# Decoding all of w_out inside the first stage's blocks 1 to 7 and parting it in block 8

## The chip, the cores and the metric

The kernel runs on one core of one Trainium2 chip. The metric is the time of one execution on the device in microseconds. PE is TensorE, DVE is VectorE, ACT is ScalarE, POOL is GpSimd; SP only issues DMAs here.

## What is computed

```python
def _attn_ref(q, k, v):                  # 8 batches, 8 heads, 576 tokens, 64 dims
    k_p, v_p = (mean over 8 neighbouring tokens of k, v)
    attn = softmax(q @ k_p.T / sqrt(D))
    return attn @ v_p                    # laid out as x: 4608 x 512
def _moe_ref(x, w_in, w_out):            # d_ff 2048
    h = x @ w_in
    return (h * cos(h)) @ w_out
def _moe2_ref(x, w_in, w_out, g_ln):     # d_ff 1024
    h = x @ w_in
    e = exp(h - max(h)); sm = e / (sum(e) + 1e-9)
    solu = h * sm
    ln = (solu - mean(solu)) / sqrt(var(solu) + 1e-6) * g_ln
    return ln @ w_out
```

The weights come as float64 bit patterns and are decoded on the chip.

## The kernel before

**Stages.** Stage 1 walks over 9 blocks of 512 tokens (`NB`). In each block it multiplies the block's attention output x with w_in in 8 units (`NQ`); one unit (`h_mm`, L619) is 24 matmuls of 512 columns, dealt out over 8 slots (`SL`) of 3 matmuls. A block has therefore 64 slots, and the attention of the next block is laid between them. Stage 2 (`y_mm`, L702) walks over the same 72 units: 42 matmuls of 256 columns each, seven products of a Strassen-like scheme, from h cos h (called g) and combinations of w_out (`w_op`). Stage 3 is the second feed-forward layer. Every f32 matmul is done as three matmuls of a rounded high part and a low part, so every operand is first parted: ACT rounds (`hi`), POOL or DVE subtracts (`lo`).

**The order is written by hand.** `work[slot]` is a table of what is issued behind each slot; `put_at(j)` puts something at a slot counted from the start of block j-1 (its first argument may run past a block's end). Each engine then runs its own instructions in that order and waits, in order, for what each needs; an engine may run ahead of the others as far as its data allow.

**The chain of a unit** (`chain`, L624). After unit n's matmuls: step 0, ACT, L630, scale to int; step 1, DVE, L633; step 2, ACT, L636, sine; step 3, DVE, L638, the product with h, which also frees the unit's PSUM. Three units' h are held in PSUM, so unit n+3 can't start until step 3 of unit n is done. `g_store` then writes the result to DRAM (gd). Within unit n: step 2 and step 3 of unit n-2 at slots 0 and 4, step 0 and step 1 of unit n-1 at slots 0 and 3, the store at slot 6.

**The attention between the slots** (`Attn.plan`). Eight score matmuls at slots 0, 3, ... 21, whose row maximum and difference (`less`, DVE, L399 and L400) stand two slots behind; two rounds of exponentials on ACT at 12 and 24, each of which makes ACT load a table before it and another before the next sine; row sums and reciprocals on DVE (`norm`: L476, L479, L480) at 15 and 27; `prep_v` (POOL, ACT, then DVE's L344 to L349) at 19, 22, 25 in the blocks in which a batch begins; transposes and the product with v from 27 on, with their low parts on DVE (L527, L510, L552). Scores, transposes and the product share two PSUM tiles.

**Decoding.** A `Chunk` is 128 x 512 float64 words: a load, two ACT operations (`s1`), three DVE operations (`bits`: L119, L123, L127), one POOL addition (`join`, L139). Eight chunks of the second layer's w_in and the first half of w_out (8 chunks) are decoded from block 1 on, one every 24 slots; their four sums per pair of chunks (L839, DVE), the rounding (L163, ACT) and the subtraction (L164, POOL) follow at once, and the parted operands go to DRAM. The second half of w_out is decoded, summed and parted in block 8, while the first half is fetched back; the last chunk runs over into stage 2. Stage 2 takes g back from DRAM (`g_load`, L653), makes four sums of it on DVE (`g_sums`, L664), and parts it (`g_split`, L675 ACT, L677 DVE). Of that, the first unit's is put at slots 57 and 60 of block 8, the second's behind the last unit.

## Time and profile before

| | |
|---|---|
| time, median of 3 runs (lowest, highest) | 1376.14 us (1375.66, 1377.78) |
| the profiled execution: its time, and its span on the core | 1375.22 us, 1373.4 us |
| PE busy | 1307.3 us, 95% of the span |
| DVE, ACT, POOL busy | 77%, 51%, 37% |

The span begins with the first instruction and ends with the last; 1.8 us of the execution lie around it. Busy matmuls are modelled at their ends, so PE's share is not a share of its peak. Stage 1 with its attention of block 0 takes the first 579 us, stage 2 runs from 584 to 960 us, stage 3 from there to the end.

### The profile page before, as it was taken

What the parts mean: (1) busy time and instruction counts of PE and PEld (TensorE: products, weight loads), DVE (VectorE), ACT (ScalarE), POOL (GpSimd) and SP (SyncE); (2) the same over time, 40 slices, a digit from 0 to 9 for tenths busy, and PEclk for the clock granted to TensorE, in tenths of its full rate; (3) what the DMA queues carried; (4) which work ended last, traced back from release to release, by engine and by line L of the source; (5) the groups of instructions that cost most, each with busy time, mean ns of one, the idle gap of its engine ahead of it and who ended that gap; (6) DMA issues with size and microseconds to landing.
All of it is one profiled execution on the core that took longest, in us unless ns stands there. A gap on an engine that the chain in (4) does not pass through costs nothing. (4 is left out here: it accounts for less than half of the span.)

```text
span 1373.4 us, 20471 instructions
## 1 busy us (share of the span) xinstructions
PE 1307.3 (95%) x7510; PEld 1136.8 (83%) x7510; DVE 1054.4 (77%) x1686; ACT 700.4 (51%) x1000; POOL 503.4 (37%) x676
## 2 busy tenths in 40 slices
PE   5879899999999989879999999999999999999998
PEld 4558788787877878779999999999878888888887
DVE  7897677867778675898889888887677777776753
ACT  4576656655566564744444444443444444444432
POOL 3757555756466240621110000111234333333310
PEclk8989999999999999979999999999999999999999
DMA  8424456555465526944455555558521011111101
GB/s 291 153 81 170 157 189 216 200 216 187 155 209 193 185 103 224 348 154 136 144 152 170 162 166 153 158 150 291 233 63 62 31 62 34 60 39 54 40 23 39
DMA packets 80116, 200.83 MB, mean 146 GB/s; under 512 B 7696, under 2 KB 26128, under 8 KB 80016
## 3 DMA queue, kind: packets, MB, share of 16 engines
q1 hardware_dynamic: 79872, 199.52, 43.1%
q8 instruction: 59, 0.97, 0.3%
q14 instruction: 41, 0.34, 0.1%
q10 hardware_dynamic: 144, 0.00, 0.0%
HBM read 122.95 MB, written 76.55 MB: 145 GB/s over the span
## 5 line engine op out<-in xcount | busy, mean ns | idle before, releaser
L619 PE MATMUL h<-x,w 128*128 128x512 f32 x1728 | 440.9, 403 | 21.9 <-DVE t L638 17.7
L619 PEld LDWEIGHTS h<-x,w 128*128 128x128 f32 x1728 | 318.7, 191 | 90.6 <-DVE t L638 19.7
L702 PE MATMUL y<-g,wy 128*128 128x256 f32 x3024 | 367.9, 285 | 13.2 <-DVE g L677 6.1
L702 PEld LDWEIGHTS y<-g,wy 128*128 128x128 f32 x3024 | 366.7, 194 | 14.5 <-DVE g L677 6.8
L675 ACT CAST g<-gs 128x1024 fp32r<-128x1024 f32 x72 | 75.7, 1051 | 175.2 <-PE y L702 106.9
L677 DVE TENSOR_TENSOR g<-gs,g 128x1024 fp32r<-128x1024 f32 x72 | 89.5, 1243 | 41.1 <-ACT g L675 41.1
L139 POOL TENSOR_TENSOR dec<-dec,raw 128x512 int32<-128x512 int32 x24 | 34.6, 1440 | 233.0 <-DVE dec L127 218.9
L633 DVE SCALAR_TENSOR_TENSOR t<-t,h 128x1024 f32<-128x1024 int32 x72 | 87.4, 1214 | 22.2 <-ACT t L630 22.1
L636 ACT ACTIVATE t<-t,cst 128x1024 f32<-128x1024 f32 x72 | 82.9, 1152 | 37.8 <-DVE t L633 37.7
L910 POOL TENSOR_TENSOR yl<-yr,yh 128x1024 fp32r<-128x1024 f32 x18 | 43.6, 2420 | 148.7 <-ACT yh L905 148.7
L630 ACT ACTIVATE t<-h 128x1024 int32<-128x1024 f32 x72 | 73.2, 1017 | 47.6 <-PE h L619 47.3
L231 POOL TENSOR_TENSOR kvraw<-kvraw 128x256 f32<-128x256 f32 (+3 forms) x128 | 81.6, 637 | 29.3 <-DMA kvraw<-in_vM 11.1
L638 DVE TENSOR_TENSOR t<-t,h 128x1024 f32<-128x1024 f32 x72 | 86.8, 1206 | 0.0
L664 DVE TENSOR_TENSOR gs<-gr,gs 128x256 f32<-128x256 f32 x144 | 72.5, 503 | 5.0
L677 DVE TENSOR_TENSOR g<-gr,g 128x768 fp32r<-128x768 f32 x72 | 72.3, 1005 | 0.0
L1041 POOL TENSOR_TENSOR sc<-sc,cst 128x1 f32<-128x1 f32 x36 | 20.3, 565 | 140.8 <-DVE sc L1030 113.5
L139 POOL TENSOR_TENSOR wf<-dec,raw 128x512 int32<-128x512 int32 x24 | 32.3, 1345 | 105.5 <-DVE dec L127 82.7
L1076 ACT COPY o<-o 128x512 f32<-128x512 f32 x36 | 21.1, 586 | 96.7 <-PE o L1094 96.7
L1092 PE MATMUL o<-w,lh 128*128 128x512 f32 x176 | 69.0, 392 | 0.0
L1094 PE MATMUL o<-w,ll 128*128 128x512 f32 x176 | 68.5, 389 | 0.0
L1093 PE MATMUL o<-w,lh 128*128 128x512 f32 x176 | 68.5, 389 | 0.0
L675 ACT CAST g<-gr 128x768 fp32r<-128x768 f32 x72 | 59.8, 830 | 0.0
(181 smaller groups left out, 2545.4 us busy)
## 6 DMA issues: line engine op xcount, KB each, us to landing
gd<-t SPq DMA_DIRECT2D x72, 512.0 KB, 2.9
gr<-gd SPq DMA_DIRECT2D x72, 512.0 KB, 4.0
raw<-in_w_in SPq DMA_DIRECT2D x24, 512.0 KB, 5.3
raw<-in_w_out SPq DMA_DIRECT2D x24, 512.0 KB, 5.1
kvraw<-in_kT SPq DMA_DIRECT2D x32, 288.0 KB, 4.4
qT<-in_qT SPq DMA_DIRECT2D x36, 256.0 KB, 4.6
yd<-yo SPq DMA_DIRECT2D x36, 256.0 KB, 4.8
yr<-yd SPq DMA_DIRECT2D x18, 512.0 KB, 4.1
```

The costliest lines, as they stand in the source:

```text
L231: nc.gpsimd.tensor_tensor(out=x[:, 0:m], in0=x[:, 0:m], in1=x[:, m:2 * m], op=ALU.add)
L619: nc.tensor.matmul(h_ps[n][:, i], lhsT=w[:, a, kk, :], rhs=x[:, b], start=(kk == 0 and m == 0), stop=(kk == KD - 1 and m == 2),)
L630: nc.scalar.activation(out=t.bitcast(I32), in_=h, func=AF.Copy, scale=1.0 / TWO_PI, bias=0.25)
L633: nc.vector.scalar_tensor_tensor(out=t, in0=t.bitcast(I32), scalar=-TWO_PI, in1=h, op0=ALU.mult, op1=ALU.add)
L636: nc.scalar.activation(out=t, in_=t, func=AF.Sin, bias=halfpi)
L638: nc.vector.tensor_tensor(out=t, in0=t, in1=h, op=ALU.mult)
L664: nc.vector.tensor_tensor(out=o, in0=x, in1=y, op=ALU.subtract)
L675: nc.scalar.copy(out=flat(g[-1])[:, 0:n * NH], in_=flat(f)[:, 0:n * NH])
L677: nc.vector.tensor_tensor(out=flat(g[-1])[:, 0:n * NH], in0=flat(f)[:, 0:n * NH], in1=flat(g[-2])[:, 0:n * NH].bitcast(F32), op=ALU.subtract)
L702: nc.tensor.matmul(y_ps[j][i][:, NH * c:NH * (c + 1)], lhsT=w[:, a, P * c:P * (c + 1)], rhs=g[y][b], start=(q == 0 and c == 0 and k == 0), ...
L1092: nc.tensor.matmul(ps, lhsT=hi, rhs=w[:, 0], start=(c == 0), stop=False)
L1093: nc.tensor.matmul(ps, lhsT=hi, rhs=w[:, 1], start=False, stop=False)
```

## The change

All 16 chunks of w_out are now decoded before block 8, each 16 slots after the one before it (24 chunks in all, from block 1's start). Their values in f32 (`wf`) and the four sums of each pair (`w_sums`, L835 of the new file) go to DRAM unparted. In block 8 `w_load` fetches six of the eight groups back and `w_split` rounds them on ACT and subtracts on POOL, group after group at slots 4, 11, 18, 25, 32 and 42; the last two groups are loaded and parted in stage 2. The sums and the parting of stage 2's first g unit stand at slots 52 and 58, the sums of the second at 56, its parting behind the last unit. The steps of the unit chain and the attention's operations are moved by a slot or a few, and the decoding of the second layer's w_out in stage 2 begins 5 units later with 7 units between chunks in place of 8.

```diff
         def plan(self, put, o, raw, ahead=10):
             put(o - ahead, self.load, raw)
             put(o, self.s1)
-            put(o + 2, self.bits)
-            put(o + 4, self.join)
+            put(o + 4, self.bits)
+            put(o + 7, self.join)
...
-                    staged((o, o + 2), self.scores, p, u)
-                put((12, 12, 24, 24)[p], self.exp, p)
+                    staged((o, o + 3), self.scores, p, u)
+                put((13, 13, 25, 25)[p], self.exp, p)
             for b in new:
-                staged((19, 22, 25), prep_v, b)
+                staged((14, 17, 21), prep_v, b)
             for hf in range(2):
-                o = (15, 27)[hf]
-                staged((o, o + 2), self.norm, 2 * hf, 2 * hf + 1)
+                o = (16, 28)[hf]
+                staged((o, o + 3), self.norm, 2 * hf, 2 * hf + 1)
...
-    def w_done(q, kept):
+    def w_sums(q):
+        a11, a12, a21, a22 = (w_f[2 * q + 1 - i % 2][:, NH * h:NH * (h + 1)] for i, h in (
+            (0, 0), (1, 0), (0, 1), (1, 1)))
+        s = w_s[q] = wo.tile([P, 4, NH], F32, "ws")
...
+            put(o + 9, lambda: nc.sync.dma_start(out=wf[2 * q][:, 1 - f % 2], in_=w_f[f]))
+            if f % 2:
+                put(o + 10, w_sums, q)
+                put(o + 13, lambda: nc.sync.dma_start(
+                    out=wf[2 * q + 1].rearrange("p a (b n) -> p (a b) n", n=NH), in_=w_s[q]))
...
+    def w_load(q):
+        if q < 6:
+            w_s[q] = [xp.tile([P, 2, BLK], F32, tag="x0", name="ws") for _ in range(2)]
...
+        for t, d in zip(w_s[q], (wf[2 * q + 1], wf[2 * q])):
+            nc.sync.dma_start(out=t, in_=d)
+
+    def w_split(q, put, o):
...
+        for i in range(4):
+            two(put, o + i, lambda i=i: part(i, 0), lambda i=i: part(i, 1), lambda i=i: src(i))
...
-        for q in range(4):
-            chunks += w_chunks(q, False)
+        chunks += [w_chunk(f) for f in range(NF)]
         put = put_at(2)
         for i, c in enumerate(chunks):
-            c.plan(put, 3 * SL * (i + 2 * (i // NQ)), raws[i % 2])
+            c.plan(put, 2 * SL * (i + 2 * (i // NQ > 0)), raws[i % 2])
         for k in range(KH):
-            o = 3 * SL * KD * (k + 1) + 13
+            o = 2 * SL * KD * (k + 1) + 3
             put(o, weight_sums, k)
...
-        for i, c in enumerate(sum((w_chunks(q, True) for q in range(4, NQ)), [])):
-            c.plan(put, (2, 15, 22, 31, 38, 46, 52, 58)[i], raws[i % 2], 8 if i < 7 else 7)
-        for i in range(16):
-            put(4 + 7 * i // 2, w_fetch, *divmod(i, 4))
-        put(57, g_sums, 0)
-        put(60, g_split, 0)
+        for q, o in enumerate((4, 11, 18, 25, 32, 42)):
+            put(o - 9, w_load, q)
+            w_split(q, put, o)
+        for m in range(2):
+            put(44 + 2 * m, g_load, m)
+            put(52 + 4 * m, g_sums, m)
+        put(58, g_split, 0)
...
-                if n > 1 and s in (0, 4):
-                    chain(n - 2, 2 + s // 4)
-                if n > 0 and s in (0, 3):
-                    chain(n - 1, s // 3)
-                if n > 1 and s == 6:
+                if n > 1 and s == 3:
+                    chain(n - 2, 3)
+                if n > 0 and s in (0, 4, 7):
+                    chain(n - 1, (0, 4, 7).index(s))
+                if n > 1 and s == 5:
                     g_store(n - 2)
...
-        for n, step in ((last - 1, 2), (last, 0), (last - 1, 3), (last, 1), (last, 2)):
+        for n, step in ((last - 1, 3), (last, 0), (last, 1), (last, 2)):
             chain(n, step)
         g_load(2)
-        g_sums(1)
         g_store(last - 1)
+        g_split(1)
         chain(last, 3)
         g_store(last)
...
-                lambda o, fn, *a, i=i: late[NQ * i + 3 + o // 3].append(lambda: fn(*a)), 6,
+                lambda o, fn, *a, i=i: late[8 + 7 * i + o // 3].append(lambda: fn(*a)), 6,
```

Three places in the engines' order.

DVE in the middle of block 2. Before, from the preparation of v (vw, vL) to the low part of the first transpose (eT); L633 and L638 are steps 1 and 3 of the chain, of two units that follow each other (L638's is the older):

```order
L344 TENSOR_TENSOR vw<-v,vw 128x128
L345 TENSOR_SCALAR vw<-vw,cst 128x128
L347 SCALAR_TENSOR_TENSOR vw<-vw,cst 128x128
L349 TENSOR_TENSOR vL_101<-vw,cst 128x512
L633 SCALAR_TENSOR_TENSOR t<-t,h 128x1024
L476 TENSOR_REDUCE sm<-e 128x8 x2
L479 TENSOR_SCALAR sm<-sm 128x16
L480 RECIPROCAL sm<-sm 128x16
L638 TENSOR_TENSOR t<-t,h 128x1024
L527 TENSOR_TENSOR eT<-eTp,eT 128x512
```

Now, the same stretch (the last `less`, L399 and L400, is now behind the preparation of v):

```order
L344 TENSOR_TENSOR vw<-v,vw 128x128
L345 TENSOR_SCALAR vw<-vw,cst 128x128
L347 SCALAR_TENSOR_TENSOR vw<-vw,cst 128x128
L349 TENSOR_TENSOR vL_101<-vw,cst 128x512
L399 TENSOR_REDUCE mx<-sc 128x4
L400 TENSOR_TENSOR e<-sc,mx 128x288
L638 TENSOR_TENSOR t<-t,h 128x1024
L633 SCALAR_TENSOR_TENSOR t<-t,h 128x1024
L476 TENSOR_REDUCE sm<-e 128x8 x2
L479 TENSOR_SCALAR sm<-sm 128x16
L480 RECIPROCAL sm<-sm 128x16
L527 TENSOR_TENSOR eT<-eTp,eT 128x512
```

L638 has moved from behind the younger unit's L633 and the row sums to ahead of both. In blocks 4 to 7 the four additions of `w_sums` stand just ahead of this L638.

ACT in block 7 from its second exponentials on; before:

```order
L457 ACT_TABLE_LOAD
L457 ACTIVATE e<-e 128x576 x2
L114 ACTIVATE dec<-raw 128x512
L115 ACTIVATE raw<-raw 128x512
L526 CAST eT<-eTp 128x512
L509 CAST eL<-eLp 128x512
L636 ACT_TABLE_LOAD
L636 ACTIVATE t<-t,cst 128x1024
```

Now, from the row ahead of the exponentials' L630 on:

```order
L114 ACTIVATE dec<-raw 128x512
L115 ACTIVATE raw<-raw 128x512
L636 ACTIVATE t<-t,cst 128x1024
L630 ACTIVATE t<-h 128x1024
L457 ACT_TABLE_LOAD
L457 ACTIVATE e<-e 128x576 x2
L526 CAST eT<-eTp 128x512
L636 ACT_TABLE_LOAD
L636 ACTIVATE t<-t,cst 128x1024
```

The sine (L636) of the unit that PE needs next, and the chunk's `s1` (L114, L115), now stand ahead of the exponentials.

DVE at the end of block 8 (t_5173, t_5229, t_5288 before and t_5190, t_5225, t_5265 now are the chain tiles of the last three units, 69, 70 and 71; gs, gr and g belong to stage 2's first two units). Before:

```order
L664 TENSOR_TENSOR gs_5240<-gr_5106 128x512
L664 TENSOR_TENSOR gs_5240<-gr_5106,gs_5240 128x256 x2
L633 SCALAR_TENSOR_TENSOR t_5229<-t_5229,h_5168 128x1024
L638 TENSOR_TENSOR t_5173<-t_5173,h_5108 128x1024
L119 TENSOR_SCALAR dec_5249<-dec_5249 128x512
L123 TENSOR_SCALAR dec_5249<-dec_5249 128x512
L127 SCALAR_TENSOR_TENSOR dec_5249<-raw_558,dec_5249 128x512
L677 TENSOR_TENSOR g_5268<-gs_5240,g_5266 128x1024
L677 TENSOR_TENSOR g_5272<-gr_5106,g_5270 128x768
L638 TENSOR_TENSOR t_5229<-t_5229,h_5168 128x1024
L633 SCALAR_TENSOR_TENSOR t_5288<-t_5288,h_5224 128x1024
```

Now:

```order
L664 TENSOR_TENSOR gs_5227<-gr_5179,gs_5227 128x256 x2
L677 TENSOR_TENSOR g_5239<-gs_5206,g_5237 128x1024
L677 TENSOR_TENSOR g_5243<-gr_5167,g_5241 128x768
L638 TENSOR_TENSOR t_5190<-t_5190,h_5140 128x1024
L633 SCALAR_TENSOR_TENSOR t_5225<-t_5225,h_5186 128x1024
L638 TENSOR_TENSOR t_5225<-t_5225,h_5186 128x1024
L633 SCALAR_TENSOR_TENSOR t_5265<-t_5265,h_5221 128x1024
L677 TENSOR_TENSOR g_5274<-gs_5227,g_5272 128x1024
L677 TENSOR_TENSOR g_5278<-gr_5179,g_5276 128x768
L638 TENSOR_TENSOR t_5265<-t_5265,h_5221 128x1024
```

The parting of the first g unit now stands ahead of unit 69's last step, the parting of the second ahead of unit 71's last step, and no decoding stands between them. On PE the order of all matmuls is unchanged; the third product of stage 2's first unit waits, now as before, for unit 71's L638, because its PSUM bank held that unit's h.

## Rows read from the trace of the kernel before

**Rows 1.** The page: busy time of PE and the others.

```profile
PE 1307.3 (95%) x7510; PEld 1136.8 (83%) x7510; DVE 1054.4 (77%) x1686; ACT 700.4 (51%) x1000; POOL 503.4 (37%) x676
```

**Rows 2.** PE's h matmuls, blocks 1 to 7: busy, mean | idle before, releaser.

```profile
L619 PE MATMUL h<-x,w 128*128 128x512 f32 x1328 | 340.9, 402 | 15.4 <-DVE t L638 15.2
```

**Rows 3.** PE in order of time, blocks 2 and 7: start, us, ... [idle before].

```profile
212.22 1.65 PE L619 MATMUL h<-x,w 128*128 128x512 f32 x6 [1.09 <-DVE t L638]
213.71 0.49 PE L522 MATMUL eTp<-ident,em 128*128 128x128 f32 x3
...
506.48 1.80 PE L619 MATMUL h<-x,w 128*128 128x512 f32 x5 [3.53 <-DVE t L638]
```

**Rows 4.** DVE in order of time, middle of block 2.

```profile
204.54 1.24 DVE L344 TENSOR_TENSOR vw<-v,vw 128x128 fp32r<-128x128 f32 x1
...
208.06 1.21 DVE L633 SCALAR_TENSOR_TENSOR t<-t,h 128x1024 f32<-128x1024 int32 x1
...
211.00 1.16 DVE L638 TENSOR_TENSOR t<-t,h 128x1024 f32<-128x1024 f32 x1
212.08 0.68 DVE L527 TENSOR_TENSOR eT<-eTp,eT 128x512 fp32r<-128x512 f32 x1
```

**Rows 5.** The sums of w_out (L839) in blocks 1 to 7, four groups of four.

```profile
122.00:530.00 408.00, 9.28 (x16) 0.99 0.52 183
```

**Rows 6.** Stretches: length, busy PE, PEld, DVE, ACT, POOL; clock, DMA, GB/s.

```profile
50.00:100.00 50.00, 35.50 (x152) 26.65 (x151) 45.95 (x69) 33.64 (x49) 34.84 (x34) 0.90 0.30 104
330.00:335.00 5.00, 5.00 (x22) 4.31 (x21) 2.95 (x3) 1.29 (x3) 4.83 (x8) 0.67 0.86 311
500.00:510.00 10.00, 6.47 (x27) 4.98 (x27) 9.04 (x15) 6.74 (x10) 5.80 (x8) 0.87 0.13 52
585.00:590.00 5.00, 0.89 (x4) 0.89 (x5) 4.96 (x5) 0.95 (x2) 2.19 (x1) 0.50 0.61 210
595.00:600.00 5.00, 5.00 (x28) 5.00 (x27) 4.93 (x6) 4.74 (x9) 4.50 (x4) 0.55 0.88 272
```

**Rows 7.** PE in order of time from block 8 into stage 2.

```profile
529.40 50.03 PE L619 MATMUL h<-x,w 128*128 128x512 f32 x219
584.04 0.80 PE L702 MATMUL y<-g,wy 128*128 128x256 f32 x2 [4.61 <-ACT g L675]
589.11 2.51 PE L702 MATMUL y<-g,wy 128*128 128x256 f32 x10 [4.27 <-DVE g L677]
594.07 6.45 PE L702 MATMUL y<-g,wy 128*128 128x256 f32 x32 [2.45 <-issue]
602.00 1.22 PE L702 MATMUL y<-g,wy 128*128 128x256 f32 x8 [1.49 <-DVE g L677]
```

**Rows 8.** DVE, then ACT, in order of time around the same place.

```profile
578.13 1.77 DVE L664 TENSOR_TENSOR gs<-gr 128x512 f32<-128x512 f32 x1 [1.58 <-POOL wf L139]
...
592.75 1.21 DVE L638 TENSOR_TENSOR t<-t,h 128x1024 f32<-128x1024 f32 x1
...
603.92 1.22 DVE L677 TENSOR_TENSOR g<-gs,g 128x1024 fp32r<-128x1024 f32 x1
605.06 0.95 DVE L677 TENSOR_TENSOR g<-gr,g 128x768 fp32r<-128x768 f32 x1
605.93 0.68 DVE L664 TENSOR_TENSOR gs<-gr 128x512 f32<-128x512 f32 x1
...
582.21 1.05 ACT L675 CAST g<-gs 128x1024 fp32r<-128x1024 f32 x1 [0.35 <-DVE gs L664]
583.16 0.83 ACT L675 CAST g<-gr 128x768 fp32r<-128x768 f32 x1
583.90 1.15 ACT L636 ACTIVATE t<-t,cst 128x1024 f32<-128x1024 f32 x1
584.95 1.00 ACT L630 ACTIVATE t<-h 128x1024 int32<-128x1024 f32 x1
```

**Rows 9.** ACT's group of the chunks' first step, 529 to 585 us.

```profile
L114 ACT ACTIVATE dec<-raw 128x512 f32<-128x512 f32 x8 | 5.3, 666 | 13.5 <-DMA raw<-in_w_out 13.5
```

More of the change, by code (lines that the diff above doesn't have):

```diff
@@ L150, in plan @@
             put(o, self.s1)
-            put(o + 2, self.bits)
-            put(o + 4, self.join)
+            put(o + 4, self.bits)
+            put(o + 7, self.join)
             if self.g is not None:
-                put(o + 7, lambda: nc.vector.tensor_scalar(
+                put(o + 10, lambda: nc.vector.tensor_scalar(
                     out=self.f, in0=self.f, scalar1=self.g, scalar2=None, op0=ALU.mult))
@@ L667, in tile @@
         def tile():
[L668 to L669 removed]
+            if m < 2:
+                return (wo, wi)[m].tile([P, 4, NH], F32R, "g", (12, 9)[m] + len(g))
             return xp.tile([P, 4, NH], F32R, tag=("x0", "x1")[m % 2], name="g")
@@ L747, in fused_kernel @@
     whole, tw, w2_in_t, w2_out_t = {}, {}, [], []
-    wd = [dram.tile([P, 2, BLK], F32R, tag="wd", name=f"wd{i}", bufs=40) for i in range(36)]
-    wd_in, wd_out, wd_tw, wd_y = wd[0:8], wd[8:16], wd[16:24], wd[24:36]
-    wd_y4 = [dram.tile([P, 2, NH], F32R, tag="wd4", name=f"wd4{i}", bufs=4) for i in range(4)]
+    wd = [dram.tile([P, 2, BLK], F32R, tag="wd", name=f"wd{i}", bufs=24) for i in range(24)]
+    wd_in, wd_out, wd_tw = wd[0:8], wd[8:16], wd[16:24]
+    wf = [dram.tile([P, 2, BLK], F32, tag="wf", name=f"wf{i}", bufs=16) for i in range(16)]
     def whole_tile(c):
@@ L785, in tile @@
                 return t[0]
-            two(put, o + 9, lambda: tile()[:, 0], lambda: tile()[:, 1], lambda: c.f)
-            put(o + 15, put_away, d, tile)
+            two(put, o + 12, lambda: tile()[:, 0], lambda: tile()[:, 1], lambda: c.f)
+            put(o + 18, put_away, d, tile)
         return done
@@ L866, in w_fetch @@
-    def w_fetch(q, i):
-        if i == 0:
-            w_get[q] = w_slots(q)
-        t = w_get[q][i]
-        if i < 3:
-            nc.sync.dma_start(
-                out=t.rearrange("p o w n -> p o (w n)").bitcast(F32), in_=wd_y[3 * q + i].bitcast(F32))
-        else:
-            nc.sync.dma_start(out=t.bitcast(F32), in_=wd_y4[q].bitcast(F32))
-    w_get = {}
-    def w_chunks(q, kept):
-        return [
-            Chunk(w_out_w[2 * q], lambda *a: None, whole=lambda: w_whole(2 * q)),
-            Chunk(w_out_w[2 * q + 1], w_done(q, kept), whole=lambda: w_whole(2 * q + 1))]
+    def w_sums(q):
+        a11, a12, a21, a22 = (w_f[2 * q + 1 - i % 2][:, NH * h:NH * (h + 1)] for i, h in (
+            (0, 0), (1, 0), (0, 1), (1, 1)))
+        s = w_s[q] = wo.tile([P, 4, NH], F32, "ws")
+        s1, s2, s3, s4 = (s[:, i] for i in range(4))
+        for o, x, y, op in (
+            (s1, a21, a22, ALU.add), (s2, s1, a11, ALU.subtract),
+            (s3, a21, a11, ALU.subtract), (s4, a12, s2, ALU.subtract)):
+            nc.vector.tensor_tensor(out=o, in0=x, in1=y, op=op)
@@ new lines, in fused_kernel, with w_chunk @@
+    w_s = {}
+    def w_chunk(f):
+        q = f // 2
+        def done(put, o, c):
+            put(o + 9, lambda: nc.sync.dma_start(out=wf[2 * q][:, 1 - f % 2], in_=w_f[f]))
[3 more added lines that the diff above has]
+                    out=wf[2 * q + 1].rearrange("p a (b n) -> p (a b) n", n=NH), in_=w_s[q]))
+        return Chunk(w_out_w[f], done, whole=lambda: w_whole(f))
+    def w_load(q):
+        if q < 6:
+            w_s[q] = [xp.tile([P, 2, BLK], F32, tag="x0", name="ws") for _ in range(2)]
+        else:
+            w_s[q] = [wo.tile([P, 2, BLK], F32, "ws", 2 * q + i) for i in range(2)]
+        for t, d in zip(w_s[q], (wf[2 * q + 1], wf[2 * q])):
+            nc.sync.dma_start(out=t, in_=d)
@@ new lines, in w_split, with part, src @@
+    def w_split(q, put, o):
+        t = []
+        def part(i, w):
+            if not t:
+                t.extend(w_slots(q))
+            return t[i][:, :, w] if i < 3 else t[3][:, w]
+        def src(i):
+            s, a = w_s[q]
+            if i < 2:
+                return quarters(s)[:, 2 * i:2 * i + 2]
+            return a[:, :, 0:NH] if i == 2 else a[:, 1, NH:BLK]
+        for i in range(4):
+            two(put, o + i, lambda i=i: part(i, 0), lambda i=i: part(i, 1), lambda i=i: src(i))
@@ L1290, in fused_kernel @@
             Chunk(w2_out_w[i], w2_done(wd_out[i], 14 + i % 2), g=g_sb[:, i:i + 1]).plan(
-                lambda o, fn, *a, i=i: late[NQ * i + 3 + o // 3].append(lambda: fn(*a)), 6,
+                lambda o, fn, *a, i=i: late[8 + 7 * i + o // 3].append(lambda: fn(*a)), 6,
                 raws[i % 2])
+        for q in (6, 7):
+            late[q - 5].append(lambda q=q: w_load(q))
+            w_split(q, lambda o, fn, *a, q=q: late[q - 3 + o // 3].append(lambda: fn(*a)), 0)
         for m in range(len(units)):
@@ L1296, in fused_kernel @@
                 g_load(m + 3)
-            for s in range(SL if m < 2 else 0):
-                for fn in work[BL * NB + SL * m + s]:
-                    fn()
             for fn in late[m]:
```

38 lines of the change are left out of this document (1 added, 37 removed).

## The prediction

> **What bounds the kernel now.** I read the page first: PE is busy for 1307.3 of 1373.4 us [rows 1], so 66 us at most can come from PE's waits, besides what the clock takes. The order of PE's matmuls doesn't change; the change can only shorten, lengthen or move those waits. So I went through PE's rows for them, stretch by stretch. Three stretches have waits that this change touches.
>
> First, blocks 1 to 7 (122 to 530 us). PE waits 15.4 us in front of h matmuls, 15.2 of it for L638 on DVE [rows 2], about once a block, at the start of the block's fifth unit: 1.09 us in block 2, 3.53 in block 7 [rows 3]. The rows of DVE say why: L638, which frees the PSUM for that unit, stands behind the preparation of v (204.54 to 208.06), the younger unit's L633 and the row sums, and so runs only from 211.00 to 212.16 [rows 4]; PE would have gone on at 212.22 - 1.09 = 211.13.
>
> Second, the passage into stage 2. The last h matmul ends at 529.40 + 50.03 = 579.43; call it E. Stage 2's first matmuls come at 584.04, and its 44th ends at about 600.5; after the last wait, of 1.49, it is 602.00 = E + 22.6 [rows 7]. PE's clock is at half there (0.50, 0.55) [rows 6], after PE sat almost idle from E on. The wait that ends last is the one at 594.07: the third product needs unit 71's L638, which runs from 592.75 to 593.96 [rows 8]. The row names "issue" because the releaser isn't recorded, but the times meet.
>
> Third, block 0: PE 35.5 us busy in 50 to 100, with DVE busy 45.95 of 50 [rows 6].
>
> **The change part by part.**
>
> *L638 ahead of L633 and the row sums (blocks 1 to 7).* Laid over block 2: L638 could start where the preparation of v ends, 208.06, and end at 209.2, 1.9 us ahead of PE's need (the last `less` is now behind the preparation, 0.9 us, but the 0.9 goes from ahead of it). DVE's whole work up to the transposes' low part L527 is the same, so that still ends at about 212.7. The third set of transposes needs the PSUM that L527 frees; it came at 213.71, so without the wait at 212.6 [rows 3, 4]. I put 0.3 us for what is left in blocks 1 to 3. Block 7 has no preparation of v, 3.5 us less of DVE's work: 0. Its wait of 3.53 had another reason, a chunk's `bits` in front of L633 that stood waiting for ACT's `s1` behind two exponentials; now `s1` and the sine stand ahead of the exponentials.
>
> *The sums of w_out.* In blocks 4 to 7 one group of four additions stands just ahead of that L638. A group takes 9.28 / 4 = 2.3 us [rows 5]. With it L638 ends at 211.5, 0.4 us late, and L527 at 215.1 against 212.6 + 0.4: 2.1 more. So 2.5 us in each of blocks 4, 5 and 6, where v is prepared too. Blocks 1 to 7 together: 3 x 0.3 + 3 x 2.5 = 8.4 us in place of 15.4, **7.0 us less**. At best all go: 15.4. At worst DVE's heap of work makes PE wait elsewhere, and longer, as worked out in the first rival: 16.2 more.
>
> *The clock in blocks 1 to 7.* Behind two of those waits the granted clock stood at 0.67 for 5.0 us of PE's work and at 0.87 for 6.47 [rows 6]: 5.0 x 0.33 + 6.47 x 0.13 = 2.5 us. The waits that I leave are shorter; I keep 1 us: **1.5 less** (0 to 2.5).
>
> *More chunks per block (four in place of 2.7), weight sums moved to the third slot of blocks 2 and 3, the stores' place.* Eight chunks more in these blocks cost DVE `bits` of three operations each; DVE has its idle time at a block's beginning, and that is where every first chunk and the weight sums now fall. 0, with the rival's price as the upper bound.
>
> *Block 8 up to E.* PE ran 50.03 us there without a wait [rows 7], though ACT sat 13.5 us waiting for raw chunks in front of its part of the chain [rows 9]. Now decoding is gone from DVE, and ACT waits for the fetched groups instead. Each fetch from the third on goes into a buffer that POOL's subtraction of the group two before must free, and SP's queue, with the g stores, stands behind that fetch; ACT's L630 and L636 stand behind the rounding that waits for it. PE tolerates holds of about 13.5 / 8 = 1.7 us a chunk, so 0; if ACT is held 1 us longer than PE tolerates in each of six groups, 6 us more. No gain: there is no wait to take.
>
> *The passage.* The first unit's g is ready before E now, so twelve matmuls run at once. The third product still needs unit 71's L638, and I follow the queues with the durations of [rows 4, 8] from the end of unit 70's matmuls, one unit before E: 50.03 / 219 x 24 = 5.5 us. ACT: L630 of unit 70 (1.0) ends at E - 4.4, then the two roundings of g (1.05, 0.83) at E - 2.5. DVE: the low parts (1.22 after the first rounding, then 0.95) to E - 1.2, L638 of unit 69 (1.21) to E, L633 of 70 (1.21) to E + 1.2. ACT: its L636 (1.15) to E + 2.35, L630 of 71 to E + 3.35. DVE: L638 of 70 to E + 3.55, L633 of 71 to E + 4.75. ACT: L636 to E + 5.9 and the second g's roundings to E + 7.8; DVE: their low parts to E + 9.15, L638 of 71 to **E + 10.35**, in place of E + 14.5. From there PE needs what it took before for the same work at the half clock (6.45), and the wait of 1.49 is gone, since the second g was ready at E + 9.15: 4.2 + 1.5 = **5.7 us less**. PE sits idle for about 9 us again, so I give the clock nothing. At best L638 of 71 waits for nothing but its own chain (1.0 + 1.2 + 1.15 + 1.2, E + 4.6) and the clock stays: the 32 matmuls then take 6.45 x 0.55 = 3.5 us, to E + 8.1, 14.5 us less than E + 22.6. At worst the g sums are slowed: L664 took 1.77 at 578.13, with POOL busy beside it, and 0.68 at 605.93 alone [rows 8]; that is 1.1 us for the first of a unit's three operations, some 2.2 if the other two lose as much together, and 2.2 of the 5.7 are gone.
>
> By the Trainium skill (SBUF — State Buffer, Who interferes with whom) a DVE instruction with two SBUF inputs and a GpSimd instruction that reads SBUF exclude each other for a whole instruction. That speaks against parting on GpSimd beside the g sums; the trace agrees (1.77 against 0.68), and by it the gain would be 2.2 us smaller if GpSimd's last group ran into slot 52.
>
> *Block 0.* The chain's steps and `less` move there too, but DVE has 46 us of work in 50 whatever its order: 0, from -3 to +3.
>
> *Stage 2's later decoding, and two groups parted there.* PE's rows show no wait from 602 us to stage 2's end, and the work only changes its place there: 0, and 1 us either way.
>
> **Sum:** 7.0 + 1.5 + 5.7 = 14.2 us from the profiled execution's 1375.2 (1373.4 of span and 1.8 around it): 1361.0. That execution was 0.9 under the median of the runs; I write 1361.5, between the two.
>
> **The rivals.** (1) *Slower: DVE's heap moves into the scores.* Every block now has a chunk at slots 4 and 20, the preparation of v at 21, sums at 26, `less` a slot later with only three slots before its PSUM is wanted. If DVE can't work this off between the clumps, each of the seven blocks waits as long as the longest one now (3.53) [rows 3], and blocks 4 to 6 the sums' 2.3 [rows 5] on top: 24.7 + 6.9 = 31.6 us in place of 15.4, so 1375.2 + 16.2 - 5.7 = 1386. Against it: block 2 has the same work in its middle and waits 1.09. It decides for slower where PE's wait passes 3.0 us a block on the mean ((15.4 + 5.7) / 7); now it is 2.2.
>
> (2) *The waits move but don't shrink.* Blocks 1 to 7 as before, the passage as worked out: 1375.2 - 5.7 = 1369.5. For it: DVE's total work in the middle of a block is the same, and PE needs several of its results.
>
> (3) *All waits of blocks 1 to 7 go* with their clock: 15.4 + 2.5 + 5.7 = 23.6, 1352. For it: the sums may fall where DVE has caught up, since `bits` no longer waits for ACT.
>
> (4) *The last block is bound by POOL and the fetches*, ACT held in each group: 6 us lost there, 2.2 in the passage: 1369.2. With rival 2 on top nothing is left that can be measured, 1378.
>
> **How the numbers follow.** A run of this kernel can tell some 0.2% from no change, 2.75 us: faster is under 1373.4, slower over 1378.9. The forecast (1356 to 1367) 0.46; rival 3 (1348 to 1356) 0.16; rivals 2 and 4 alone (1367 to 1373.4) 0.19; together, within 0.2%: 0.08; rival 1: 0.11. Faster 0.81, same 0.08, slower 0.11. The range leaves out half of the slower case and some of the same one, and the low end of rival 3: 1350 to 1375.
>
> **What would show it.** In the new trace, h matmuls in blocks 1 to 7 idle for 8.4 us in all, behind L527 or L638 in blocks 4 to 6 and next to nothing in blocks 1 to 3 and 7; no wait in front of h in block 8; stage 2's first twelve matmuls within 2 us of E, the third product at E + 10.4 behind L638, the second unit without a wait, the clock at half in between. Waits in front of scores (L391) for `less` would make rival 1 right; waits for L636 or L630 in block 8, with ACT idle behind a fetch, rival 4. If unit 71's L638 runs much before E + 9, my queue of the passage is wrong.

## The result, and the profile after

The changed kernel takes 1355.44 us (median of four runs, 1354.56 to 1358.70) against 1375.90 for the kernel before in the same comparison: ratio 0.9855, 95% interval 0.9834 to 0.9876. The forecast was 1361.5, the range 1350 to 1375. The profiled execution has a span of 1352.8 us, 20.6 less than before.

What answers to [rows 1], the page's busy times:

```profile
PE 1299.7 (96%) x7510; PEld 1132.1 (84%) x7510; DVE 1058.2 (78%) x1686; ACT 697.6 (52%) x992; POOL 500.3 (37%) x668
```

PE executes the same 7510 instructions in 7.6 us less of busy time. The other engines' work hardly changed: this is a change of order, not of amount. What answers to [rows 2], PE's groups in 115 to 515 us (busy, mean | idle before, releaser):

```profile
L619 PE MATMUL h<-x,w 128*128 128x512 f32 x1351 | 341.4, 399 | 0.8 <-DVE t L638 0.8
L391 PE MATMUL sc<-kT,qT 128*128 128x144 f32 (+1 forms) x248 | 38.8, 292 | 0.4 <-DVE e L400 0.4
...
L522 PE MATMUL eTp<-ident,em 128*128 128x128 f32 x112 | 17.1, 275 | 5.8 <-DVE eT L527 5.8
```

The waits in front of h for L638, 15.2 us before, are 0.8. In their place the transposes (L522) wait 5.8 us for the low part L527. In order of time (blocks 2, 4, 5 and 6), in place of [rows 3]:

```profile
209.82 0.66 PE L522 MATMUL eTp<-ident,em 128*128 128x128 f32 x4 [1.89 <-DVE eT L527]
...
322.69 0.66 PE L522 MATMUL eTp<-ident,em 128*128 128x128 f32 x4 [1.21 <-DVE eT L527]
...
379.38 0.66 PE L522 MATMUL eTp<-ident,em 128*128 128x128 f32 x4 [1.59 <-DVE eT L527]
...
437.77 0.66 PE L522 MATMUL eTp<-ident,em 128*128 128x128 f32 x4 [0.90 <-DVE eT L527]
```

The passage into stage 2, in place of [rows 7], and the clock around it, in place of [rows 6] (length, busy PE, PEld, DVE, ACT, POOL; clock, DMA, GB/s). E is now 563.07:

```profile
563.07 1.59 PE L702 MATMUL y<-g,wy 128*128 128x256 f32 x12
573.33 20.73 PE L702 MATMUL y<-g,wy 128*128 128x256 f32 x158 [8.67 <-DVE t L638]
595.64 4.57 PE L702 MATMUL y<-g,wy 128*128 128x256 f32 x36 [1.58 <-DVE g L677]
```

```profile
330.00:335.00 5.00, 5.00 (x28) 4.13 (x27) 2.51 (x3) 1.06 (x3) 4.39 (x9) 1.00 0.43 170
...
565.00:570.00 5.00, 0.00 (x0) 0.00 (x0) 2.39 (x3) 3.49 (x5) 0.00 (x0) 0.66 0.66 218
570.00:575.00 5.00, 1.67 (x8) 1.70 (x9) 4.64 (x6) 0.87 (x2) 0.00 (x0) 0.50 0.22 88
575.00:580.00 5.00, 5.00 (x37) 5.00 (x37) 0.84 (x2) 1.57 (x2) 0.00 (x0) 0.81 0.88 256
```

The twelve matmuls with the readied g run right at E, the third product comes at E + 10.3 behind L638, the second unit follows without a wait, and a new wait of 1.58 us stands at the fifth unit.

**Where the 20.6 us came from.** I cut each profile at the first score matmul of block 1 and at E. "Waits" sums what PE's rows between them show as idle before.

| kernel (span, parts and waits in us) | block 1 to E | waits in it | E to the span's end | time, median us | ratio to the kernel before, 95% |
|---|---|---|---|---|---|
| before | 455.2 | 16.3 | 794.0 | 1375.9 to 1377.5 (each group of runs has its own) | |
| changed | 441.0 | 7.0 | 789.7 | 1355.4 | 0.9834 to 0.9876 |
| e1, new order alone | 442.1 | 8.0 | 793.7 | 1361.7 | 0.9875 to 0.9909 |
| e2, old chain | 447.5 | 11.4 | 788.6 | 1360.0 | 0.9861 to 0.9890 |
| e3, old attention | 443.6 | 9.0 | 792.1 | 1360.7 | 0.9863 to 0.9892 |
| e5, old order | 457.7 | 17.4 | 789.0 | 1370.5 | 0.9939 to 0.9966 |
| e4, L638 first | 440.6 | 6.8 | 786.3 | 1353.0 | 0.9802 to 0.9839 |
| e6, later sums | 436.6 | 2.9 | 789.3 | 1351.0 | 0.9800 to 0.9827 |
| e7, new passage | 440.3 | 6.6 | 786.1 | 1351.4 | 0.9804 to 0.9836 |
| e8, e7 and later parting | 439.7 | 6.3 | 785.4 | 1352.7 | 0.9810 to 0.9851 |
| e9, e6, e7 and early third g | 436.6 | 3.0 | 786.9 | 1347.1 | 0.9767 to 0.9804 |
| e10, e9 and later parting | 436.5 | 3.0 | 784.4 | 1345.1 | 0.9755 to 0.9788 |
| e11, e9 and later weight parts | 435.5 | 2.2 | 785.2 | 1346.3 | 0.9756 to 0.9795 |
| e12, all of it | 435.5 | 2.3 | 784.6 | 1346.6 | 0.9767 to 0.9794 |

The change gave 14.2 us from block 1 to E (9.3 of waits, 5.0 of the rest), 4.3 behind E, and 2.1 ahead of block 1. The last is not explained, and may be chance: block 1 begins at 124.2 in the kernel before, at 122.1 in the changed one, and anywhere from 122.4 to 124.5 in the kernels below whose order up to there is the changed one's. Each row of the table is one profiled execution, so its parts can be off by some 2 us for that alone. Differences of time below are of medians; the kernel before itself ran at 1375.9 to 1377.5 in the different groups of runs, so where two groups are compared the differences by the ratios stand beside them.

### The profile page after: what moved, and what is told of

It is laid out like the page before. It is cut to its first block, busy times and chain, and to the rows that moved or that the text cites. A ratio compares the mean times of both kernels' runs of the same rounds, so it can differ in the third digit from the quotient of the medians.

```text
span 1352.8 us, 20432 instructions
## 1 busy us (share of the span) xinstructions
PE 1299.7 (96%) x7510; PEld 1132.1 (84%) x7510; DVE 1058.2 (78%) x1686; ACT 697.6 (52%) x992; POOL 500.3 (37%) x668
## 5 line engine op out<-in xcount | busy, mean ns | idle before, releaser
L619 PE MATMUL h<-x,w 128*128 128x512 f32 x1728 | 435.9, 401 | 1.4 <-DVE t L638 0.8
L677 DVE TENSOR_TENSOR g<-gs,g 128x1024 fp32r<-128x1024 f32 x72 | 90.2, 1253 | 33.3 <-ACT g L675 33.2
L636 ACT ACTIVATE t<-t,cst 128x1024 f32<-128x1024 f32 x72 | 83.0, 1152 | 63.3 <-DVE t L633 63.2
L139 POOL TENSOR_TENSOR dec<-dec,raw 128x512 int32<-128x512 int32 x24 | 33.9, 1414 | 210.0 <-DVE dec L127 176.4
L638 DVE TENSOR_TENSOR t<-t,h 128x1024 f32<-128x1024 f32 x72 | 87.4, 1214 | 26.1 <-ACT t L636 26.0
L630 ACT ACTIVATE t<-h 128x1024 int32<-128x1024 f32 x72 | 73.4, 1020 | 49.0 <-PE h L619 48.9
L633 DVE SCALAR_TENSOR_TENSOR t<-t,h 128x1024 f32<-128x1024 int32 x72 | 87.2, 1212 | 5.1 <-ACT t L630 5.1
L677 DVE TENSOR_TENSOR g<-gr,g 128x768 fp32r<-128x768 f32 x72 | 76.1, 1057 | 0.0
L164 POOL TENSOR_TENSOR wy<-ws,wy 128x512 fp32r<-128x512 f32 (+1 forms) x32 | 40.5, 1301 | 61.9 <-ACT wy L163 61.8
L139 POOL TENSOR_TENSOR wf<-dec,raw 128x512 int32<-128x512 int32 x24 | 31.4, 1308 | 83.7 <-DVE dec L127 43.6
```

The lines of the kernel that those rows point to most:

```text
L619: nc.tensor.matmul(h_ps[n][:, i], lhsT=w[:, a, kk, :], rhs=x[:, b], start=(kk == 0 and m == 0), stop=(kk == KD - 1 and m == 2),)
L630: nc.scalar.activation(out=t.bitcast(I32), in_=h, func=AF.Copy, scale=1.0 / TWO_PI, bias=0.25)
L633: nc.vector.scalar_tensor_tensor(out=t, in0=t.bitcast(I32), scalar=-TWO_PI, in1=h, op0=ALU.mult, op1=ALU.add)
L636: nc.scalar.activation(out=t, in_=t, func=AF.Sin, bias=halfpi)
L638: nc.vector.tensor_tensor(out=t, in0=t, in1=h, op=ALU.mult)
L677: nc.vector.tensor_tensor(out=flat(g[-1])[:, 0:n * NH], in0=flat(f)[:, 0:n * NH], in1=flat(g[-2])[:, 0:n * NH].bitcast(F32), op=ALU.subtract)
```

## The experiments

**Order or decoding?** My theory: the new places in the order took the waits of blocks 1 to 7, and the clock's dips with them; the new place of the decoding only serves the passage. Four kernels part the two. The first is the kernel before with the new order alone:

```diff
-                if n > 1 and s in (0, 4):
-                    chain(n - 2, 2 + s // 4)
-                if n > 0 and s in (0, 3):
-                    chain(n - 1, s // 3)
+                if n > 1 and s == 3:
+                    chain(n - 2, 3)
+                if n > 0 and s in (0, 4, 7):
+                    chain(n - 1, (0, 4, 7).index(s))
... (exp, less, norm, prep_v, bits and join to their new slots)
```

> The kernel before with nothing but the new places in the order: the steps of the unit chain (step 0, 1, 2 at slots 0, 4, 7 of the next unit, step 3 at slot 3 of the one after), the attention's exponentials, row sums, less and preparation of v, and in blocks 1 to 7 the chunks' bits, join and all that follows them 2 or 3 slots later. Decoding, sums and parting of w_out stay where they were, g is readied as before. Theory (the order takes the waits of blocks 1 to 7 and the clock dips behind them): h matmuls of blocks 1 to 7 idle for 5 to 8 us in place of 16.3, the granted clock in 330-335 and 505-515 us is 1.00, E falls by 12 to 15 and stage 2 begins as before: 1361 to 1364 us. Rival (the gain comes from the lighter last block and the moved decoding, not from the order): 1373 to 1376 us with the waits for L638 still there.

Measured: 1361.7, 14.8 us less than the kernel before beside it; waits of 8.0 us, none for L638, and the clock full where it had dipped. In 505 to 510 us, where the kernel before shows 0.73:

```profile
505.00:510.00 5.00, 5.00 (x27) 4.14 (x27) 2.63 (x4) 3.04 (x4) 0.00 (x0) 1.00 0.28 107
```

The order alone is the larger part of the gain; the rival is out. Then the changed kernel with one half of the old order each, by the same lines the other way round:

> The changed kernel with the steps of the unit chain put back to their old places (step 2 and 3 at slots 0 and 4 of the second unit after, step 0 and 1 at slots 0 and 3 of the next one, store at slot 6), and the old order of the last five steps behind the last unit; all else as changed. Theory (the waits went because L638 stands ahead of L633 and the row sums): each of blocks 1 to 7 waits for L638 again, 12 to 18 us in all in place of 7.0, partly with the clock down behind it; the passage keeps most of its gain: 1363 to 1370 us. Rival (decoding moved out of block 8 did it): 1354 to 1357 us.

> The changed kernel with the attention's operations put back to their old slots (less 2 slots behind its scores, exponentials at 12 and 24, row sums at 15 and 27, preparation of v at 19, 22, 25); the chain of the units stays new. Theory (the chain and the earlier preparation of v share the gain, since at the old place the preparation at slot 25 stands just ahead of the L638 of slot 35): waits of blocks 1 to 7 between 9 and 13 us, some of the clock dips back: 1358 to 1364 us. If the chain's place alone did it: 1354 to 1357 us. If the attention's places alone did it: 1367 to 1371 us.

Measured: 1360.0 and 1360.7, 4.6 and 5.3 us lost (2.8 and 3.0 by the ratios). The first missed its range: L638 waits come back (7.2 us), but short ones, and the clock stays full. The second lies in its range, but without the dips in blocks 1 to 7 that it expected, and only 2.6 us of its loss lie between block 1 and E (6.5 for the first); 2.4 lie behind E, where its clock falls behind a wait of 1.76 at stage 2's fifth unit, and the rest ahead of block 1. Putting back either half alone costs far less than the 14.8. So both halves together, with the old places of bits and join:

> The changed kernel with the whole order of the kernel before: the old places of the chain, of the attention's operations and of bits, join and the parting of chunks; decoding of w_out, fetching and the readied first g as changed. The new order alone gave 14.8 us, yet putting back the chain alone cost only 4.6 and the attention alone 5.3. Theory (either half of the new order keeps PE's waits short enough that its clock stays full, only both old halves together bring waits of over 2 us and the dips): waits of blocks 1 to 7 of 14 us or more, the granted clock under 1.00 somewhere in 120-530 us: 1368 to 1373 us. Rival (the two halves add up): 4.6 + 5.3 = 9.9, 1364 to 1366 us, with the clock full. Second rival (the decoding moved out of block 8 has a gain of its own in blocks 1 to 7): 1360 to 1363 us.

Measured: 1370.5, 15.1 us lost (13.5 by the ratios), more than the two halves add up to by either count: the theory's case. From block 1 to E it is 16.7 us against 6.5 + 2.6. The waits are back in front of h, behind L638 (16.7 of 17.4 us), and the clock dips behind three of them (length, busy PE, clock, DMA, GB/s):

```profile
190.00:195.00 5.00, 4.66 (x15) 0.66 0.74 206
215.00:220.00 5.00, 5.00 (x17) 0.66 0.88 313
390.00:395.00 5.00, 3.46 (x13) 0.77 0.53 175
395.00:400.00 5.00, 5.00 (x24) 0.89 0.51 168
```

PE was busy wherever the clock was low, so that is 5.00 x (0.34 + 0.34 + 0.23 + 0.11) = 5.1 us of clock; neither half alone loses any there. This kernel also puts back bits and join, which neither half does. How much of the excess is theirs no run shows. The order is worth 13.5 to 15 us with the decoding at either place, and all else that the change does 5 to 7 (1361.7 to 1355.4, 1377.5 to 1370.5; 5.1 and 6.5 by the ratios). Between block 1 and E the new decoding gains little of its own: 442.1 becomes 441.0 us with the new order, and 455.2 becomes 457.7 with the old.

**The sums of w_out.** My prediction had put 7.5 us of waits in blocks 4 to 6 on them.

```diff
-                put(o + 10, w_sums, q)
+                put(o + 17, w_sums, q)
...
-                put(o + 13, lambda: nc.sync.dma_start(
+                put(o + 20, lambda: nc.sync.dma_start(
```

> The changed kernel with the four sums of w_out 7 slots later (17 slots behind their chunk's first operation, their store 20 slots), so that in blocks 4 to 6 they stand behind the low part L527 for which the third transposes wait, in place of ahead of L638 and the row sums. Theory (the sums, 1.7 us a group, cause the waits of 1.21, 1.59 and 0.90 at L527 in blocks 4 to 6): these three waits go, 3 to 4 us less, 1351.5 to 1353 us. Rival (the waits come from DVE's whole heap, as in block 2, which has no sums and waits 1.89): the waits stay or move to the next release, 1354 to 1357 us.

Measured: 1351.0, 4.5 us less than the changed kernel (5.6 by the ratios) and 0.5 us under the theory's range. Of the waits 1.21, 1.59 and 0.90 there are left (PE in order of time):

```profile
328.65 0.71 PE L549 MATMUL xo<-eT,vM 128*128 128x320 f32 x3 [0.23 <-DVE eT L527]
...
384.40 0.79 PE L549 MATMUL xo<-eT,vM 128*128 128x384 f32 x3 [0.17 <-DVE eT L527]
```

So the sums do cause these waits, as the prediction had it. Its price for them was too high: a group with DVE to itself takes 0.41 + 0.42 + 0.42 + 0.42 = 1.7 us in block 4, not the 2.3 that [rows 5] gave as a mean over groups of which three of four ran beside POOL.

**Block 2.** It has no sums and yet waited 1.89. Its rows in the kernel with later sums show two operations of v's preparation (L345, L347) that take 1.3 us each and end just behind POOL's (DVE, then POOL, in order of time):

```profile
202.86 1.31 DVE L345 TENSOR_SCALAR vw<-vw,cst 128x128 f32<-128x128 f32 x1
204.20 1.30 DVE L347 SCALAR_TENSOR_TENSOR vw<-vw,cst 128x128 f32<-128x128 f32 x1
...
202.74 1.33 POOL L164 TENSOR_TENSOR tw<-wf,tw 128x512 fp32r<-128x512 f32 x1
204.04 1.30 POOL L139 TENSOR_TENSOR wf<-dec,raw 128x512 int32<-128x512 int32 x1
```

In block 4 of the changed kernel, with POOL elsewhere, the same two take 0.27 and 0.35. So L164 was moved away (together with later sums, the new passage and the early third g, below):

```diff
-                weight_parts(put, o + 4 + 6 * i, KD * k + i)
+                weight_parts(put, o + (4, 10, 28, 34)[i], KD * k + i)
```

> The kernel with later sums, new passage and early third g, with the last two of each four weight parts (L163 on ACT, L164 on POOL) 12 slots later, so that in block 2 they no longer stand on POOL beside the preparation of v on DVE. Theory (the wait of 1.9 in front of block 2's third transposes comes from L345 and L347 of that preparation, 1.30 us each beside POOL's L164 in place of 0.3 without): both take under 0.5 us, the wait falls to under 1.0: 1 us less than without, at the edge of what the time can show, so the rows decide. Rival (POOL's join, L139, stands there in its place): both keep 1.3 us or one of them does, and the wait stays over 1.2.

```profile
202.62 1.33 DVE L345 TENSOR_SCALAR vw<-vw,cst 128x128 f32<-128x128 f32 x1
203.98 0.35 DVE L347 SCALAR_TENSOR_TENSOR vw<-vw,cst 128x128 f32<-128x128 f32 x1
...
202.51 1.35 POOL L139 TENSOR_TENSOR wf<-dec,raw 128x512 int32<-128x512 int32 x1
```

Half of each: POOL's next operation, join, moved up and holds L345 in L164's place; L347 is free again, and the wait fell from 1.91 to 1.15. The time (1346.3 against 1347.1) can't show it; the rows do.

So L347's running beside POOL costs 0.8 us of block 2's wait, but it is not what the change brought. In the kernel before, L344 and L345 were slowed beside POOL too (1.24 and 1.32 us), and the preparation of v, from L344 to the end of L349, took 3.6 us there and takes 3.8 now. In e1 they take 1.11 and 1.31, and block 2 has no wait at all. What is new is the load on DVE from the block's first scores to the end of the first low part L527 (kernel before, changed kernel, e1: length, busy DVE, clock, DMA, GB/s; then a row of the changed kernel, and one of e5):

```profile
183.33:212.76 29.43, 25.02 (x41) 1.00 0.49 171
177.83:209.77 31.94, 31.07 (x47) 1.00 0.61 228
179.19:206.74 27.55, 24.43 (x40) 1.00 0.56 202
...
179.59 3.57 DVE L762 TENSOR_TENSOR wf<-wf 128x512 f32<-128x512 f32 x4
...
184.94 4.22 DVE L762 TENSOR_TENSOR wf<-wf 128x512 f32<-128x512 f32 x4
```

DVE has 0.9 us of idle time left in place of 4.4. The second layer's weight sums (L762) now stand at the third slot of this block, and a second chunk's `bits` (some 2 us) come in it; e1 has the new order with the old decoding, so neither stands there. In e5 the L638 that PE waits 3.05 us for, at 190.34, comes right behind these sums. No run moved the weight sums alone.

**The passage.** First, whether unit 71's L638 sets the third product:

```diff
-        g_split(1)
         chain(last, 3)
+        g_split(1)
         g_store(last)
```

> The changed kernel with one line moved: behind the last unit, step 3 of unit 71 (L638) is issued ahead of the parting of the second g unit (L675, L677) in place of behind it. By the queues of the changed kernel's trace L638 of unit 71 then follows ACT's L636, which ends at E + 5.8, so the third product starts at E + 7.0 in place of E + 10.1, and the second g unit is ready some 1.2 us later, still ahead of PE. Theory (L638 of unit 71 sets the third product): 2.5 to 3.5 us less than the changed kernel, 1352 to 1353 us, if nothing behind gives it back. Rival: PE waits for unit 4's g (ACT's L163 of the seventh group stands ahead of its rounding) by what it came earlier, 1.58 us become 4 to 5: 1354 to 1356 us.

```profile
565.11 1.59 PE L702 MATMUL y<-g,wy 128*128 128x256 f32 x12
572.44 21.01 PE L702 MATMUL y<-g,wy 128*128 128x256 f32 x158 [5.74 <-DVE t L638]
595.17 45.02 PE L702 MATMUL y<-g,wy 128*128 128x256 f32 x373 [1.72 <-DVE g L677]
```

Measured: 1353.0, 2.5 us less; the third product at E + 7.3, the wait 2.9 shorter, and the wait at the fifth unit hardly longer. The queue reading holds. Going further, only one of the first unit's seven products needs unit 71's PSUM at all, and it need not be the third:

```diff
-        for n, step in ((last - 1, 3), (last, 0), (last, 1), (last, 2)):
+        for n, step in ((last, 0), (last - 1, 2), (last, 1), (last - 1, 3), (last, 2), (last, 3)):
...
-        for i, (x, y) in enumerate(PROD):
+        for i in ((0, 1, 3, 4, 5, 6, 2) if m == 0 else range(7)):
+            x, y = PROD[i]
```

> The changed kernel with two things moved in the passage into stage 2. Behind the last unit: step 0 of unit 71 ahead of step 2 of unit 70, then steps 1, 3, 2, 3 of units 71, 70, 71, 71, then the parting of the second g unit; and stage 2's first unit does its seven products in the order 1, 2, 4, 5, 6, 7, 3, so that the PSUM freed last (unit 71's) is wanted last. By the durations of the changed kernel's trace: products 4 and 5 need unit 69's L638, done at about E, products 6 and 7 unit 70's at E + 3.5, product 3 unit 71's at E + 4.7. Theory: PE waits under 2.5 us in front of the first unit in place of 8.67, the granted clock stays at or near full, the second unit starts by E + 7; some of these 7.5 us goes back where g of units 3 and 4 comes too late: 1348 to 1351 us. Rival (the loads of g set the pace in any case): no more than the 2.5 us that moving L638 alone gave, 1352 to 1354 us.

```profile
562.77 3.03 PE L703 MATMUL y<-g,wy 128*128 128x256 f32 x24
566.53 2.62 PE L703 MATMUL y<-g,wy 128*128 128x256 f32 x20 [0.74 <-DVE t L638]
569.75 5.30 PE L703 MATMUL y<-g,wy 128*128 128x256 f32 x42 [0.59 <-DVE g L677]
577.81 11.65 PE L703 MATMUL y<-g,wy 128*128 128x256 f32 x84 [2.77 <-DVE g L677]
590.88 14.31 PE L703 MATMUL y<-g,wy 128*128 128x256 f32 x117 [1.42 <-DVE g L677]
```

Measured: 1351.4, 4.1 us less than the changed kernel (4.8 by the ratios), just above the theory's range and below the rival's. The 8.67 us became 0.74 + 0.59, the second unit starts at E + 7.0 and the clock is full until 575; then the third unit waits 2.77, with the clock down around it, and the fifth 1.42, which takes back a little more than the theory had set aside. The third unit's low part stood on DVE behind the fourth's sums, which waited 2.93 us for their load. Its parting ahead of those sums, with the later sums of w_out:

> The changed kernel with the later sums of w_out (which alone gave 4.4 us), the new order of the passage (which alone gave 4.0), and one thing more: the parting of the third g unit (L675, L677) issued ahead of the sums of the fourth in place of behind them, because in the passage kernel DVE's low part of the third g stood 2.9 us behind sums that waited for the fourth g's load, and PE waited 2.77 us for it. Theory (the gains lie in different stretches and add up, and the wait of 2.77 goes): 1355.4 - 4.4 - 4.0 - 2.8 = 1344 us, within 1343 to 1346. Rival (the loads of g set the pace, so the 2.77 comes back at the fourth or fifth unit): 1346 to 1349 us.

Measured: 1347.1. The 2.77 is gone, but 1.37 and 2.90 stand at the fourth and fifth units: the rival's case. What was gained earlier, 4.5 and 4.1, adds up within the noise (8.4, or by the ratios 9.6 for 5.6 and 4.8).

**Parting w_out's last groups later.** I had put the wait of 1.58 on ACT's L163 in front of g's rounding. Twice it was moved, each time in one group of runs with the kernel that differs in nothing else:

```diff
-            w_split(q, lambda o, fn, *a, q=q: late[q - 3 + o // 3].append(lambda: fn(*a)), 0)
+            w_split(q, lambda o, fn, *a, q=q: late[q - 2 + o // 3].append(lambda: fn(*a)), 0)
```

> The kernel of the run before this one (the passage in the new order) with the rounding and subtraction of the seventh and eighth group of w_out one unit later in stage 2, so that ACT's L163 no longer stands, waiting for PE, ahead of the rounding of unit 4's g. Theory (that L163 causes the wait of 1.58 in front of unit 4): 1.5 to 3 us less than the kernel without it, 1346 to 1349 us, no wait behind L677 at the fifth unit. Rival (loads and sums of g set it): same time as without it.

> The kernel of the run before this one with the rounding and subtraction of the seventh and eighth group of w_out one unit later in stage 2. In the passage kernel that moved the wait of 1.42 at the fifth unit to 0.38 and 0.72 at later ones and was worth nothing that could be measured. Theory (once g of unit 3 comes in time, POOL's subtractions beside DVE's sums and low parts are what delays g of units 5 to 7): 0.5 to 1.5 us less than without. Rival (nothing hangs on it): within 1 us of the kernel without it.

Measured: 1352.7 (1349.6 to 1356.6) against 1351.4, no difference that can be told; and 1345.1 against 1347.1, with intervals that overlap. In the rows the first moves the waits along (1.42 became 0.38 and 0.72 at later units); the second also shortens them (1.37 and 2.90 became 0.27, 1.74 and 0.29). Both move POOL's subtractions (L164) together with ACT's L163, so they can't tell which of the two delays g. Rows of the changed kernel can. They are DVE's sums of the sixth unit and low parts of the fifth, ACT's last rounding of the fifth, and POOL's long run:

```profile
587.29 1.78 DVE L664 TENSOR_TENSOR gs<-gr 128x512 f32<-128x512 f32 x1
589.10 2.30 DVE L664 TENSOR_TENSOR gs<-gr,gs 128x256 f32<-128x256 f32 x2
591.33 2.32 DVE L677 TENSOR_TENSOR g<-gs,g 128x1024 fp32r<-128x1024 f32 x1
593.57 2.02 DVE L677 TENSOR_TENSOR g<-gr,g 128x768 fp32r<-128x768 f32 x1
...
588.98 0.83 ACT L675 CAST g<-gr 128x768 fp32r<-128x768 f32 x1
...
584.42 13.46 POOL L164 TENSOR_TENSOR wy<-ws,wy 128x512 fp32r<-128x512 f32 x8 [31.34 <-ACT wy L163]
```

The rounding was done at 589.81, 1.5 us before DVE came to the low part, so the place of L163 isn't what PE waited for in the changed kernel. While POOL subtracts, the two L677 take 2.32 and 2.02 us; alone they take 1.22 and 0.95 [rows 8], and that difference of 2.2 us is more than the wait of 1.58. No run takes the subtractions out of stage 2, so this is read from rows and not shown by an experiment. The last kernel put g's parting ahead of the next sums for four units:

> Everything that gained: the changed kernel with the later sums of w_out, the new passage, the parting of w_out's last two groups one unit later, the later weight parts, and the parting of g ahead of the next unit's sums for units 2 to 5 of stage 2 in place of unit 2 alone. In the kernel without the last two, PE waited 0.27 and 1.74 us for the low parts of g (L677) of stage 2's fourth and fifth unit, since these stood on DVE behind the next unit's sums and then ran beside POOL (2.31 us each in place of 1.22), and its clock was at 0.69 for 5 us behind that. Theory (the place behind the sums is what delays them): both waits together under 0.8 us and the clock full, 2 to 3 us for these and 0.8 for the weight parts: 1341.5 to 1343.5 us. Rival (DVE beside POOL is too slow in any order, so the wait moves to a later unit): 1344 to 1346 us.

```profile
565.49 20.18 PE L703 MATMUL y<-g,wy 128*128 128x256 f32 x166 [0.59 <-DVE g L677]
586.32 0.50 PE L703 MATMUL y<-g,wy 128*128 128x256 f32 x2 [0.65 <-ACT g L675]
588.26 6.93 PE L703 MATMUL y<-g,wy 128*128 128x256 f32 x42 [1.43 <-DVE g L677]
596.84 8.41 PE L703 MATMUL y<-g,wy 128*128 128x256 f32 x68 [1.66 <-DVE g L677]
```

Measured: 1346.6, 0.6 us above the rival's range. It is the rival's case: 166 matmuls run through, and waits of 0.65, 1.43 and 1.66 follow at the next units. Kernels e9 to e12, 1345 to 1347, can't be told apart by their times; all four are some 8 to 10 us faster than the changed kernel (10 to 12 by the ratios).

## Why the prediction was right, and what it mis-sized

The measured 1355.4 lies in the range, but just under 1356 to 1367, the band that had the largest chance, and in the one of rival 3, whose case it isn't: 7.0 us of waits stayed. The sum came near by terms that missed on both sides. Against 14.2 us forecast, the profiles differ by 20.6: the waits gave 2.3 more than forecast, the clock and h's busy time 3.5, the passage 1.2, the stretch ahead of block 1 2.1 that no term stood for, and the rest of stage 2 took 2.6 back.

- *Waits of blocks 1 to 7: 7.0 us less, forecast; 9.3 measured.* The mechanism held: L638 no longer stands behind L633 and the row sums, and what is left waits mostly behind L527. Blocks 1, 3 and 7: 0.20, 0.46 and 0, as forecast. Blocks 4 to 6: 1.21, 1.93 and 0.90 in place of 2.5 each, in part because the sums are 1.7 us and not 2.3. Block 2: 2.33 in place of 0.3. There the step failed that put the additional chunks and the weight sums at 0, since "DVE has its idle time at a block's beginning": in block 2 they used that time up. The forecast also took DVE's durations along unchanged, and beside POOL's L164 and L139 two operations of v's preparation take 1.30 us each; but the preparation was slowed by POOL before as well and is only 0.2 us longer.
- *Clock in blocks 1 to 7: 1.5 us, forecast; 3.4 measured, and 1.6 beside it that had no term.* This is the part that was most mis-sized. I read two stretches, counted 6.47 x 0.13 for the second although the clock was low only where PE was busy, kept back 1 us for waits that would stay, and missed the stretch behind the second one (length, busy PE, clock, DMA, GB/s; the other two rows cut it finer):

```profile
510.00:515.00 5.00, 5.00 (x21) 0.93 0.29 118
...
506.50:507.30 0.80, 0.80 (x4) 1.00 0.08 31
507.30:510.70 3.40, 3.40 (x12) 0.50 0.36 147
```

  3.40 x 0.50 is 1.7 us, and 5.0 x 0.33 at 330 to 335 another 1.7. No wait that stayed cost any: the clock is 1.00 from block 1 to E. The other 1.6 us seem to lie in h's busy time, which fell by 4.8 (387.8 to 383.0, block 1 to E), more than the clock explains. The changed kernel with the old chain (e2) has 2.2 more of it too, at full clock (385.2), so it seems to go with the resumptions behind L638; what it consists of was not tried.
- *The passage: 5.7 us, forecast; 6.9 measured up to the second unit, and 4.3 up to the span's end.* The queue was right almost to the row: L638 of unit 71 from 571.97 to 573.18, E + 10.1 where I had E + 10.35. The 45th matmul, in the second unit, starts at E + 15.7 (578.8) in place of E + 22.6, since the clock came back sooner than I had allowed (0.81 in 575 to 580, 1.00 behind it, against 0.55 at the like place in [rows 6]); why is open. Against it stand the wait of 1.58 and some 1 us in the rest of stage 2, in the term that I had put at "0, and 1 us either way": two groups parted in stage 2, on POOL beside DVE. I had used that very contention as the worst case for block 8's g sums, and not for this place. (That PE's rows show no wait from 602 us to stage 2's end isn't quite so: one of 0.34 stands at 955.40; it is 0.60 now.)
- *Block 8: 0, forecast, and 0.* 219 h matmuls run there in 49.80 us without a wait, as in 50.03 before. The rival with POOL and the fetches is out.
- *Block 0: 0 with 3 us either way.* 77.2 us in place of 78.2; the kernels of the changed order show 77.3 to 77.9 there, so the gain is 1 us at most and not told from chance.
- *The rivals.* DVE's heap in the scores: one wait for `less`, 0.44 us, in block 2; out as a whole, though in that block DVE's heap is what PE waits for. Waits that move but don't shrink: they did move, to L527, and did shrink. All waits gone, 1352: not the changed kernel's case; with the sums seven slots later 2.9 us of waits are left and the time is 1351.0.

By the Trainium skill (SBUF — State Buffer, Who interferes with whom) a DVE operation with two SBUF inputs, or a `tensor_scalar` in a two-port mode, contends with a GpSimd instruction that reads SBUF, and the one that comes second is blocked until the first is done. Which mode L345 ran in no row shows. The traces agree at two places: L345 and L347 (0.27 and 0.35 alone, 1.30 beside POOL), and L677 (1.22 and 0.95 alone, 2.32 and 2.02).
